# Attention remade ahead of two expert layers: transposes of both heads at once, a mask added by TensorE, other loads and another step order

## The chip, the cores and the metric

The kernel runs on one core of a Trainium2 chip. The core has five engines that run their own instruction lists in order and meet only at semaphores: TensorE (PE, with its weight loads as PEld), VectorE (DVE), ScalarE (ACT), GpSimd (POOL) and SyncE (SP), which here issues every DMA. The metric is the device time of one execution in microseconds. The kernel before takes 1068.88 us (median of 3 runs, 1068.88 to 1069.41).

## The reference

Three layers follow each other; the change touches the first and the beginning of the second.

```python
# attention: batch 2, 8 heads, 576 positions, head size 64
q_d, k_d, v_d = (x.reshape(B, H, S // 4, 4, D).mean(axis=3) for x in (q, k, v))
out_up = np.repeat(softmax(q_d @ k_d.T / 8) @ v_d, 4, axis=2)        # coarse part
scores = np.where(abs(i - j) < 4, q @ k.T / 8, -1e9)                 # local part: a band 7 wide
x = out_up + softmax(scores) @ v                                     # 1152 tokens of 512 numbers
# 8 experts, all of them for every token, weights P from 8 rounds of row and column scaling
for e in range(8): out += P[:, e:e + 1] * (np.maximum(x @ w1[e], 0) @ w2[e])   # 512 -> 1024 -> 512
# last layer, mish between two products: 512 -> 2048 -> 512
```

## The kernel before, in words

Products that matter for precision are made of f16 pairs: a number is scaled by a power of two, cut into a high and a low f16 half, and each product takes three matmuls (high by high, high by low, low by high). So every weight matrix is first measured (a maximum over it gives the scale), then split into halves.

Attention works on pairs of heads, four pairs to a batch, numbered 0 to 3 in batch 0 and 4 to 7 in batch 1. For a pair the steps are: load q, k, v (`LQ`, `LV`) and 128 overlapping windows of v (`LW`); transpose q and k with TensorE (`TP`, line 501) and copy them from PSUM to the layout `qt`, `kt` (`TE`, line 514, on ACT); sum groups of four columns (`SQ`, `SK`); the local scores as 24 little products for a window of 24 queries each (`QL`); the coarse scores (`QD`, line 544); mask and maximum (`MK`, on DVE); subtract, exponentiate, sum and divide (`SUB`, `EL`, `LS`, `LN`); transpose in 32 by 32 blocks (`TR`) and spread into a block diagonal `bd` (`BD`); the same for the coarse part (`DM`, `ED`, `DS`, `DN`, `AP`, `AE`); the products with v (`AV`, `AD`); the sum of both parts, scaled (`UP`, `XF`), and its two f16 halves in `x` (`XH`, `XL`).

All instructions stand in an order written out by hand: the string `ORDER` is a list of such step names with their arguments, and each step issues its instructions to its engines when its name comes. Between the steps of attention stand those of the first expert: `W` for the measuring and splitting of w1 of expert 0 (`first_gen`: eight reduces on DVE at line 175, then for eight pieces a scaling on DVE at 191, the high half on ACT at 192 and the low half on POOL at 193), `Y` for w2 of expert 0, `Z` for measuring w1 of expert 1, `GP` for the gate's weights. When batch 0's `x` is there, the first expert begins on it: `M` (12 matmuls, line 757, into one of two PSUM banks), `R` (ACT empties the bank, line 763), `H` (DVE makes both halves of `h`, lines 768 and 769), and then `N` (its second product, line 790).

So three stages can be told apart in what follows. Stage 1 runs from the start to the first `M`: attention of batch 0 and the split of w1. Stage 2 runs from there to the end of `ORDER`: the first expert on batch 0 beside the attention of batch 1. Stage 3 is the first expert's first product on batch 1, with the gate in it. After that come the remaining experts and the last layer, which the change does not touch.

Of the kernel before, what the change touches and what calls it, by code (L numbers as in the profile page):

```python
# [10 lines left out]
F32 = mybir.dt.float32  # L11
# [10 lines left out]
def attn_moe_moe2_kernel(ctx: ExitStack, tc: tile.TileContext, q, k, v, w_gate, w1, w2, w_in, w_out, out):  # L22
    nc = tc.nc
# [16 lines left out]
    HSC2 = 2.0 ** -26  # L40
    CW = 512
# [70 lines left out]
    max_ps = [None]  # L112

    def all_max_gen(m):

        if not max_ps[0]:
            ma = all_max(m)
            yield
            yield
            return ma  # L120
        ma = Max(m, max_ps[0]())
        yield
        ma.row()
        yield
        return ma.spread()

# [31 lines left out]
    class Split:  # L158


        def __init__(self, name, srcs, slot, spare=0):
            self.name, self.srcs, self.slot, self.spare = name, srcs, slot, spare
            self.raw = []

        def load(self):
            for src in self.srcs:
                r = rawp.tile([128, 2048], F32, tag="raw", name="raw")
                nc.sync.dma_start(out=r.rearrange("p (a b) -> p a b", a=src.shape[1]), in_=src)
                self.raw.append(r)

        def scale_gen(self):
            mx = sm.tile([128, 8], F32, tag="mx", name="mx")
            for i, r in enumerate(self.raw):
                for c in range(4):
                    nc.vector.tensor_reduce(out=mx[:, 4 * i + c:4 * i + c + 1], in_=r[:, c * 512:(c + 1) * 512],
                                            axis=AX.X, op=ALU.max, apply_absolute_value=True)
                    yield
            m1 = sm.tile([128, 1], F32, tag="m1", name="m1")
            nc.vector.tensor_reduce(out=m1, in_=mx, axis=AX.X, op=ALU.max)
            ma = yield from all_max_gen(m1)  # L180
            self.s, self.inv = scale_from_max(ma, "sc_" + self.name, self.spare)
            yield

        def first_gen(self):

            self.tiles()
            yield from self.scale_gen()
            for i in range(8):
                o = slice(i * 512, (i + 1) * 512)
                rr = self.raw[i // 4][:, (i % 4) * 512:(i % 4 + 1) * 512]  # L190
# [3 lines left out]
                yield  # L194
            self.raw = []
# [5 lines left out]
        def split_gen(self):  # L201
# [16 lines left out]
            self.raw = []  # L218
# [151 lines left out]
    def w1_split(e):  # L370

        return (SplitSq if e > 1 else Split)(f"w1_{e}", [w1[e, i * 256:(i + 1) * 256, :].rearrange("(k p) f -> p k f", p=128)
                                 for i in range(2)], "wa", 2)

    def w2_split(e):

        return (Split if e == 0 else SplitSq)(f"w2_{e}", [w2[e, i * 512:(i + 1) * 512, :].rearrange("(k p) d -> p k d", p=128)
                                 for i in range(2)], "wb")


    ident = const.tile([128, 128], F32, name="ident")
    ones = const.tile([128, 128], F32, name="ones")
    ss = const.tile([128, B, 2 * NP], F32, name="ss")
# [6 lines left out]
    acc = accp.tile([128, NTT, DM], F32, name="acc")  # L390
    w_in32, w_out32 = w_in.bitcast(I32), w_out.bitcast(I32)
# [6 lines left out]
    def emit_consts(mask):  # L398
        make_identity(nc, ident)
        nc.vector.memset(ones, 1.0)  # L400
        nc.vector.memset(ss, 0.0)
        nc.gpsimd.memset(mask, 0.0)
        for j in range(4):
            for g0, g1, off in ([(0, 1, 0), (1, G, 3)] if j == 0 else
                                [(0, G - 1, 3), (G - 1, G, 8)] if j == 3 else [(0, G, 3)]):
                mk = mask[32 * j:32 * j + 32, g0:g1, :]

                nc.gpsimd.affine_select(out=mk, in_=mk, pattern=[[0, g1 - g0], [1, 32]], compare_op=ALU.is_ge,
                                        fill=-8e9, base=3 - off, channel_multiplier=-1)
                nc.gpsimd.affine_select(out=mk, in_=mk, pattern=[[0, g1 - g0], [-1, 32]], compare_op=ALU.is_ge,  # L410
                                        fill=-8e9, base=3 + off, channel_multiplier=1)


    xs = [None, None]

    class Attention:
# [4 lines left out]
        def load_m(self, src, j, tag, name):  # L421

            t = self.p[tag].tile([HM, 2, 2, 4, D], F32, tag=tag, name=name)
            nc.sync.dma_start(out=t.rearrange("p h a r d -> p (h a) (r d)"),
                              in_=src[self.b, 2 * j:2 * j + 2].rearrange("h (a p r) d -> p (h a) (r d)", a=2, r=4))
            return t

        def load_qk(self, j):
            self.qm[j] = self.load_m(q, j, "qk", "qm")
            self.km[j] = self.load_m(k, j, "qk", "km")  # L430

        def load_vm(self, j):
            self.vm[j] = self.load_m(v, j, "vm", "vm")

        def load_vw(self, j):
# [4 lines left out]
            vb = v[self.b, 2 * j:2 * j + 2]  # L440

            def win(jj, i0, i1):
                base = v[self.b, 2 * j, 0:32, :]
                src = bass.AP(tensor=base.tensor, offset=base.offset + (24 * jj - 3 + 96 * i0) * D,
                              ap=[[D, 32], [96 * D, i1 - i0], [1, D]])
                nc.sync.dma_start(out=tv[32 * jj:32 * jj + 32, i0:i1, :], in_=src)


            win(0, 1, 2 * G)
            win(3, 0, 2 * G - 1)  # L450
            win(1, 0, 2 * G)
            win(2, 0, 2 * G)
            nc.sync.dma_start(out=t[0:32, :, 0, :], in_=vb[:, 0:32, :].rearrange("h s d -> s h d"))
            nc.sync.dma_start(out=t[96:128, :, G - 1, :], in_=vb[:, S - 32:S, :].rearrange("h s d -> s h d"))
# [3 lines left out]
        def VSQ(self, j):  # L458
            vv = self.vm[j].rearrange("p h a r d -> p h (a r d)")
            junk = self.p["w2"].tile([HM, 512], F32, tag="w2", name="junk")  # L460
            for i in range(2):
                nc.scalar.activation(out=junk, in_=vv[:, i, :], func=AF.Square,
                                     accum_out=ss[0:HM, self.b, 2 * j + i:2 * j + i + 1])

        def VP(self, j):
            t = self.vm.pop(j)
            v2 = self.p["w2"].tile([HM, 512], F32, tag="w2", name="v2")
            v2 = v2.rearrange("p (h a r d) -> p h a r d", h=2, a=2, r=2)
# [9 lines left out]

        def VSM(self, j):
            self.vmax.row()  # L480

        def VSB(self, j):
            b = self.b

# [857 lines left out]
```

## Time and profile before

| | us |
|---|---|
| median of 3 runs | 1068.88 |
| the profiled execution | 1070.91 |
| its span, first to last instruction | 1069.1 |
| PE busy in the span | 1019.4 |
| DVE busy | 608.2 |
| ACT busy | 508.6 |
| POOL busy | 74.8 |

The span is the profiled execution without the 1.8 us around it. Of the span all but the first four of forty slices show PE busy at nine tenths or more, so what an edit in the first part is worth has to be read from that part alone. Times below count from the start of the span. A row that names a releaser after an arrow says what ended the idle time in front of an instruction.

### The profile page before, as it was taken

To read this page: it belongs to the slowest core of one execution; us is meant where nothing else is said; L and a number is where in the kernel's file an instruction comes from. 1 tells how busy PE (TensorE), PEld (TensorE's weight loads), DVE (VectorE), ACT (ScalarE), POOL (GpSimd) and SP (SyncE) were. 2 spreads that over 40 slices of the span, in tenths; PEclk is the share of its full clock that TensorE was granted. 3 is DMA by queue.
4 is the path that set the end of the run, shared out by engine and by line. 5 is a ranking of instruction groups with operands and counts; after the bars stand their busy time and mean duration, and the time that the engine had idled before them with its cause. 6 is when DMAs were issued, how large, how long until landed. Compare 5 with 4: busy or idle time off the path is not lost.

```text
span 1069.1 us, 18210 instructions
## 1 busy us (share of the span) xinstructions
PE 1019.4 (95%) x7545; PEld 695.5 (65%) x7545; DVE 608.2 (57%) x1312; ACT 508.6 (48%) x907; POOL 74.8 (7%) x102
## 2 busy tenths in 40 slices
PE   3777899999998999999999999999999999999998
PEld 2555656667447746754774675477467566888897
DVE  3686893732575376458338645654864336555541
ACT  5867742327526633762663475266437222334431
POOL 2463240000000000000000000000000000000000
PEclk9558899999999999999999999999999999999999
DMA  7637210200451244215123521412320440200010
GB/s 189 123 57 165 56 40 2 67 13 1 158 190 47 79 126 131 79 39 199 30 80 96 170 79 41 158 60 79 117 90 1 174 191 1 80 21 17 6 60 31
DMA packets 70211, 89.40 MB, mean 84 GB/s; under 512 B 16624, under 2 KB 54512, under 8 KB 68848
## 3 DMA queue, kind: packets, MB, share of 16 engines
q1 hardware_dynamic: 70128, 88.24, 26.7%
q8 instruction: 59, 0.97, 0.4%
q14 instruction: 24, 0.20, 0.1%
HBM read 73.29 MB, written 14.94 MB: 83 GB/s over the span
## 4 chain that ended last, share of the span: by engine, by line
PE 73%; DVE 11%; DMA 3%; ACT 3%; issue 2%; POOL 0%; ACTq 0%; POOLq 0%; SPq 0%
PE mm L757 33%; PE mm L790 21%; PE mm L1124 9%; PE n L1191 8%; DMA scr<-st 2%; DVE wal L221 1%; ACT junk L232 1%; DVE acc L805 1%; DVE w L293 1%; DVE w L290 1%; DVE m L297 1%; DMA scri<-st 1%; DVE w L286 1%; DVE w L284 1%; DVE h L769 1%
## 5 line engine op out<-in xcount | busy, mean ns | idle before, releaser
L757 PE MATMUL mm<-x,wah 128*128 128x288 f16 x2048 | 383.1, 289 | 9.2 <-ACT r L763 5.6
L790 PE MATMUL mm<-wbh,h 128*128 128x512 f16 x1152 | 350.6, 379 | 0.0
L757 PE MATMUL mm<-x,wal 128*128 128x288 f16 x1024 | 295.4, 288 | 0.0
L790 PEld LDWEIGHTS <-h 128*128 128x128 f16 x1728 | 168.2, 98 | 195.0 <-issue 1.1
L757 PEld LDWEIGHTS <-wah 128*128 128x128 f16 x2048 | 201.3, 99 | 64.1 <-issue 10.3
L790 PE MATMUL mm<-wbl,h 128*128 128x512 f16 x576 | 218.3, 379 | 0.2 <-DVE wbl L221 0.2
L781 DVE TENSOR_TENSOR h<-rr,h 128x1152 f16<-128x1152 f32 x49 | 66.5, 1358 | 152.8 <-ACT h L783 152.8
L779 ACT ACTIVATE rr<-mm 128x288 f32<-128x288 f32 x224 | 90.5, 407 | 121.2 <-PE mm L757 120.4
L757 PEld LDWEIGHTS <-wal 128*128 128x128 f16 x1024 | 101.1, 99 | 26.5
L1124 PE MATMUL mm<-xc,win 128*128 128x256 f16 (+1 forms) x960 | 107.6, 262 | 0.0
L1124 PEld LDWEIGHTS <-win 128*128 128x128 f16 x960 | 87.2, 98 | 13.3
L1133 ACT ACTIVATE tt<-mm,cf 128x512 f32<-128x512 f32 (+1 forms) x40 | 25.8, 645 | 113.1 <-PE mm L1124 111.3
L1140 DVE TENSOR_TENSOR tt<-tt 128x128 f32<-128x128 f32 x128 | 31.6, 288 | 68.8 <-ACT tt L1133 67.7
L783 ACT ACTIVATE h<-rr 128x1152 f16<-128x1152 f32 x56 | 65.0, 1161 | 1.5
L94 POOL PARTITION_ALL_REDUCE ma<-m x25 | 11.4, 454 | 701.1 <-DVE m L236 419.6
L232 ACT ACTIVATE junk<-raw 128x1024 bf16<-128x1024 f32 x52 | 54.5, 1048 | 5.4 <-DMA raw<-in_moe_w_dram 5.4
L805 DVE SCALAR_TENSOR_TENSOR acc<-mm,pc,acc 128x512 f32<-128x512 f32 x63 | 45.9, 745 | 6.5 <-PE mm L790 6.3
L1191 PEld LDWEIGHTS <-g 128*128 128x128 f16 x432 | 42.1, 98 | 5.0
L221 DVE SCALAR_TENSOR_TENSOR wbl<-raw,sc_w,wbh 128x1024 f16<-128x1024 f32 x32 | 40.6, 1306 | 0.0
L322 DVE TENSOR_TENSOR st<-w,st 128x512 f16<-128x512 f32 x32 | 22.1, 690 | 32.5 <-ACT st L321 32.0
L321 ACT ACTIVATE st<-w 128x512 f16<-128x512 f32 x32 | 19.3, 621 | 42.6 <-DMA scr<-st 37.4
L272 ACT ACTIVATE w<-f 128x512 f32<-128x512 f32 x32 | 20.8, 668 | 36.0 <-DMA f<-in_moe_w_out_dram 35.4
(188 smaller groups left out, 1069.1 us busy)
## 6 DMA issues: line engine op xcount, KB each, us to landing
raw<-in_moe_w_dram SPq DMA_DIRECT2D x32, 1024.0 KB
f<-in_moe_w_in_dram SPq DMA_DIRECT2D x16, 512.0 KB
f<-in_moe_w_out_dram SPq DMA_DIRECT2D x16, 512.0 KB
scr<-st SPq DMA_DIRECT2D x32, 256.0 KB
scri<-st SPq DMA_DIRECT2D x16, 256.0 KB
win<-scri SPq DMA_DIRECT2D x2, 2048.0 KB
qm<-in_q_dram SPq DMA_DIRECT2D x8, 288.0 KB
km<-in_k_dram SPq DMA_DIRECT2D x8, 288.0 KB
```

The source lines that it names most:

```text
L221: nc.vector.scalar_tensor_tensor(out=self.lo[:, o], in0=rr, scalar=self.s, in1=self.hi[:, o], op0=ALU.mult, op1=ALU.subtract)
L232: nc.scalar.activation(out=junk, in_=r[:, c * 1024:(c + 1) * 1024], func=AF.Square, accum_out=mx[:, 2 * i + c:2 * i + c + 1])
L757: nc.tensor.matmul(self.ps, lhsT=wt[:, ws], rhs=x[:, xi, kk, o:o + CH], start=(n == 0), stop=(n == 3 * KT - 1))
L779: nc.scalar.activation(out=r[:, c * CH:(c + 1) * CH], in_=g.ps, func=AF.Relu, scale=HSC)
L781: nc.vector.tensor_tensor(out=low[1][:, 1, :], in0=low[0], in1=low[1][:, 0, :], op=ALU.subtract)
L783: nc.scalar.activation(out=h[ft][:, 0, :], in_=r, func=AF.Copy)
L790: nc.tensor.matmul(ps, lhsT=h[ft][:, hi, t * 128:(t + 1) * 128], rhs=wt[:, ws], start=(ft == 0 and n == 0), stop=(ft == FT - 1 and n == 2))
L805: nc.vector.scalar_tensor_tensor(out=a, in0=ps, scalar=pc[:, t:t + 1], in1=a, op0=ALU.mult, op1=ALU.add)
L1124: nc.tensor.matmul(ps[:, q_ * n:(q_ + 1) * n], lhsT=win[q_][:, wi, f, ws], rhs=x[:, xi, kk, :], start=(m == 0), stop=(m == 3 * KT - 1))
L1133: nc.scalar.activation(out=tt[:, 0:2 * n], in_=ps, func=AF.Mish, scale=coef[c][:, f:f + 1])
L1140: nc.vector.tensor_tensor(out=a[o], in0=a[u], in1=a[v], op=op)
L1191: nc.tensor.matmul(ps, lhsT=gt(c, f)[:, gi, a, :], rhs=wout[b][:, wi, f, :], start=(k == f == n == 0), stop=(k == len(terms) - 1 and f == ...
```

## The change

What it does:

- Loads of q and k: four DMAs of a quarter each in place of one, into a tile of 72 rows that holds the two heads of a position beside each other, so one transpose turns both heads (`load_qk`). Each piece that a DMA moves is then 256 bytes long; before it was 1 KB.
- `TP` writes its four transposes into PSUM columns that stand four apart, so that the result lies in the order of positions. `TQ` (ACT) and `TK` (ACT or DVE) then copy 288 neighbouring numbers; `TE` is gone.
- The mask is made by DVE with arithmetic; the identity too, without the `affine_select` of POOL. It is added by a bf16 matmul of the identity with the mask, into which the 24 little products accumulate; `MK`'s addition goes. `SUB` becomes `SU` on DVE, straight from PSUM. `kt` has three zero columns in front and five behind.
- Windows of v run on into the next head (the mask closes them), so the two extra DMAs at the edges (lines 453 and 454) go.
- w1 and w2 of expert 0 and w1 of expert 1 are measured by squares on ACT, in quarters; the split of w1 is an ACT and a DVE instruction for each quarter.
- Steps name their engine (`:A`, `:V`, `:G`); `H` makes the high half of two chunks at once and `I` the low half; scratch tiles lie in `acc` and `h`.
- `ORDER` is another list.

What it moves. The first place is ACT at the start of attention, after its table load. The names `qt` and `kt` are the transposed tiles, `ad` the coarse softmax. Before:

```order
L514 ACTIVATE qt_183<-at 64x2x2x72 x2
L514 ACTIVATE kt_185<-at 64x2x2x72 x4
L514 ACTIVATE qt_183<-at 64x2x2x72 x2
L514 ACTIVATE qt_184<-at 64x2x2x72 x4
L514 ACTIVATE kt_186<-at 64x2x2x72 x4
L462 ACTIVATE junk,ss<-vm 72x512 x2
L620 ACTIVATE ad,dsu<-at,dnm 72x144 x4
```

Now, at the same place:

```order
L536 ACTIVATE qt_133<-at 128x288 x2
L439 ACTIVATE kt_135<-at 64x288 x2
L439 ACTIVATE kt_136<-at 64x288 x3
L536 ACTIVATE qt_134<-at 128x288
L645 ACTIVATE ad,dsu<-at,dnm 72x144 x4
```

Sixteen strided copies stood ahead of the first exponentials; now there are eight contiguous ones, and part of the `kt` copies is on DVE.

The second place is DVE at the end of stage 1, from the largest value of w1 to the `xf` of the fourth pair. Before:

```order
L179 TENSOR_REDUCE m_848<-mx 128x1
L683 SCALAR_TENSOR_TENSOR xf<-at,sx_607,up 128x288 x2
L106 TENSOR_REDUCE mrow<-at 1x1
L63 TENSOR_SCALAR mc<-at 128x1
L65 TENSOR_SCALAR ei<-mc 128x1
L71 TENSOR_SCALAR ab<-ei 128x1
L72 TENSOR_SCALAR ab<-ei 128x1
L73 TENSOR_SCALAR sc_w_0_880<-ab 128x2
L191 TENSOR_SCALAR raw<-raw,sc_w_0_880 128x512 x3
L587 STREAM_TRANSPOSE atl<-sl 128x384
L598 COPY bd_191<-atl 32x12x24 x2
L191 TENSOR_SCALAR raw<-raw,sc_w_0_880 128x512 x4
```

Now, from the scale of w1 (`sc_w_0`) on, with `wal` its low half:

```order
L75 TENSOR_SCALAR sc_w_0_803<-ab 128x2
L619 STREAM_TRANSPOSE acc<-sl 128x384
L441 COPY kt_135<-at 64x288 x2
L441 COPY bd_141<-acc 32x12x24 x2
L222 SCALAR_TENSOR_TENSOR wal<-raw,sc_w_0_803,wah 128x1024
L706 SCALAR_TENSOR_TENSOR xf<-at,sx_686,h 128x288 x2
L222 SCALAR_TENSOR_TENSOR wal<-raw,sc_w_0_803,wah 128x1024 x2
L706 SCALAR_TENSOR_TENSOR xf<-at,sx_686,h 128x288 x2
L222 SCALAR_TENSOR_TENSOR wal<-raw,sc_w_0_803,wah 128x1024
```

The scale of w1 is now there before the third pair's `xf`, one pair earlier, and the eight scalings and eight POOL subtractions are four DVE instructions.

The third place is DVE at the beginning of stage 3, where `gx`, `L` and `m` belong to the gate, whose maximum TensorE turns next. Before:

```order
L768 CAST h<-r 128x288
L769 TENSOR_TENSOR h<-r,h 128x288
L840 TENSOR_SCALAR gx<-invx,sc_wg 128x9
L841 TENSOR_REDUCE L<-lp 128x72
L842 TENSOR_TENSOR L<-L,gx 128x72
L844 TENSOR_REDUCE m_2122<-L 128x1
L768 CAST h<-r 128x288
```

Now:

```order
L887 TENSOR_SCALAR gx<-invx,sc_wg 128x9
L888 TENSOR_REDUCE L<-lp 128x72
L889 TENSOR_TENSOR L<-L,gx 128x72
L891 TENSOR_REDUCE m_2025<-L 128x1
L807 TENSOR_TENSOR h<-r,h 128x576
```

No half of `h` stands ahead of the gate's maximum any more.

The diff, cut to its core:

```diff
-        def load_m(self, src, j, tag, name):
...
-            nc.sync.dma_start(out=t.rearrange("p h a r d -> p (h a) (r d)"),
-                              in_=src[self.b, 2 * j:2 * j + 2].rearrange("h (a p r) d -> p (h a) (r d)", a=2, r=4))
+        def load_qk(self, src, j):
+
+            t = self.p["qk"].tile([HM, 2, 4, 2, D], F32, tag="qk", name="qk")
+            for a in range(2):
+                for h in range(2):
+                    nc.sync.dma_start(out=t[:, a, :, h], in_=src[self.b, 2 * j + h, 288 * a:288 * a + 288]
+                                      .rearrange("(p r) d -> p r d", r=4))
...
-            for a in range(2):
-                for i in range(2):
-                    c = (2 * a + i) * HM
-                    nc.tensor.transpose(ps[:, c:c + HM], t[:, par, a, 2 * i:2 * i + 2, :].rearrange("p r d -> p (r d)"),
-                                        ident[0:HM, 0:HM])
...
+            ps = self.at()[:, 0:288]
+            o = ps.rearrange("c (p r) -> c r p", r=4)
+            for r in range(4):
+                nc.tensor.transpose(o[:, r, :], t[:, i, r].rearrange("p h d -> p (h d)"), ident[0:HM, 0:HM])
...
+        def TQ(self, j, i):
+            nc.scalar.activation(out=keep["qt"][j % 2][:, 288 * i:288 * i + 288], in_=self.st["T", j, 0, i],
+                                 func=AF.Copy, scale=QSC)
+
+        def TK(self, j, i, h, eng):
+            c = slice(64 * h, 64 * h + 64)
+            copy_on(eng, keep["kt"][j % 2][c, h, 3 + 288 * i:291 + 288 * i], self.st["T", j, 1, i][c])
...
+                nc.tensor.matmul(sl[:, 0:384], lhsT=ident16, rhs=mask.rearrange("p g h c -> p (g h c)"), start=True,
+                                 stop=False)
...
-                                 rhs=kt[:, :, k0:k0 + 32], start=True, stop=True, tile_position=(0, 32 * jj))
+                                 rhs=kt[:, :, 24 * n:24 * n + 32], start=False, stop=(n >= 20),
+                                 tile_position=(0, 32 * jj))
...
-            nc.sync.dma_start(out=t[0:32, :, 0, :], in_=vb[:, 0:32, :].rearrange("h s d -> s h d"))
-            nc.sync.dma_start(out=t[96:128, :, G - 1, :], in_=vb[:, S - 32:S, :].rearrange("h s d -> s h d"))
...
-                nc.vector.tensor_scalar(out=rr, in0=rr, scalar1=self.s, scalar2=None, op0=ALU.mult)
-                nc.scalar.activation(out=self.hi[:, o], in_=rr, func=AF.Copy)
-                nc.gpsimd.tensor_tensor(out=self.lo[:, o], in0=rr, in1=self.hi[:, o], op=ALU.subtract)
...
+            if eng == "A":
+                nc.scalar.activation(out=spare_act, in_=r, func=AF.Square, accum_out=self.mx[:, i:i + 1])
...
+        def high(self, i):
+            if not hasattr(self, "hi"):
+                self.tiles()
+            nc.scalar.activation(out=self.hi[:, i * 1024:(i + 1) * 1024], in_=self.quarter(i), func=AF.Copy,
+                                 scale=self.s)
...
-        make_identity(nc, ident)
...
+        nc.vector.transpose(out=row, in_=col)
+        nc.vector.tensor_tensor(out=d, in0=col, in1=row, op=ALU.subtract)
+        for i in range(4):
+            p = slice(32 * i, 32 * i + 32)
+            nc.vector.tensor_scalar(out=ident[p, p], in0=d[p, :], scalar1=0.0, scalar2=None, op0=ALU.is_equal)
...
-        "LQ0 TP0.1 TP0.3 LQ1 TP0.2 TP0.0 TE0.1 TE0.3 LV0 TP1.2 TE0.2 TE0.0 LV1 LQ2 SK0 SQ0 TP1.1 TP1.3 TP1.0 QL0.0 "
...
+        "LQ0 LK0 LK1 TP0.0.1 TP0.0.0 TQ0.1 TQ0.0 LK2 TP0.1.0 SQ0:V TP0.1.1 TK0.0.1:A TK0.0.0:V TK0.1.0:A TK0.1.1:V "
...
```

## Rows read from the trace of the kernel before

**Rows 1.** Stages: us, length, busy us (instructions) of each engine, PE clock, DMA, GB/s:

```profile
0.00:11.33 11.33, 0.00 (x0) 0.00 (x0) 3.44 (x9) 1.28 (x1) 0.73 (x7) 1.00 0.67 156
11.33:80.15 68.82, 49.35 (x470) 36.31 (x470) 45.71 (x112) 51.62 (x119) 33.87 (x43) 0.63 0.54 118
80.15:166.00 85.85, 76.25 (x703) 48.18 (x702) 67.27 (x146) 55.41 (x129) 28.14 (x27) 0.90 0.32 82
166.00:196.93 30.93, 28.66 (x283) 22.42 (x282) 17.29 (x63) 7.12 (x17) 0.00 (x0) 0.94 0.01 2
196.93:1069.10 872.17, 865.17 (x6095) 588.58 (x6092) 474.45 (x985) 393.12 (x642) 12.06 (x27) 1.00 0.25 83
```

**Rows 2.** Waits of PE in stage 1: us in total, times, longest:

```profile
PE at L501 <- POOL ident masks.py:199: 11.3, 1, 11.3
PE at L661 <- ACT bd L596: 5.0, 2, 3.7
PE at L669 <- ACT atd L651: 1.7, 2, 1.2
PE at L501 <- ACT kt L514: 1.5, 1, 1.5
```

**Rows 3.** POOL by line, up to 169 us:

```profile
L193 POOL TENSOR_TENSOR wal<-raw,wah 128x512 f16<-128x512 f32 x8 | 9.7, 1231 | 2.3 <-ACT wah L192 2.3
...
masks.py:199 POOL TENSOR_SCALAR_AFFINE_SELECT ident<-ident 128x128 f32<-128x128 f32 x1 | 0.3, 283 | 10.1 <-issue 10.1
```

**Rows 4.** PE in order of time: start, us, line, tiles, [idle before, releaser]:

```profile
17.73 1.08 PE L537 MATMUL at<-kt,qt 128*32 128x64 f32 x32 [2.04 <-ACT qt L514]
...
80.15 0.69 PE L757 MATMUL mm<-x,wah 128*128 128x288 f16 x2
```

**Rows 5.** Waits of PE in stage 2:

```profile
PE mm L757 <- ACT r L763: 5.6, 3, 2.4
PE at L102 <- DVE mv L476: 3.0, 1, 3.0
```

**Rows 6.** Waits of PE in stage 3:

```profile
PE gm L102 <- DVE m L844: 2.3, 1, 2.3
```

**Rows 7.** ACT by line, stage 1: instructions, busy us, mean ns, idle before:

```profile
L514 ACT ACTIVATE kt<-at 64x288 f32<-64x288 f32 x20 | 13.6, 681 | 0.4
L514 ACT ACTIVATE qt<-at 64x288 f32<-64x288 f32 x16 | 10.8, 678 | 10.4 <-PE at L501 10.1
```

**Rows 8.** ACT by line, stage 2, and the page's row of another measuring:

```profile
L763 ACT ACTIVATE r<-mm 128x288 f32<-128x288 f32 x16 | 6.5, 410 | 8.0 <-PE mm L757 4.8 <-DVE h L769 2.5 <-ACT r L763 0.3
...
L232 ACT ACTIVATE junk<-raw 128x1024 bf16<-128x1024 f32 x52 | 54.5, 1048 | 5.4 <-DMA raw<-in_moe_w_dram 5.4
```

**Rows 9.** DMA from 2 to 6 us: packets, and share of 16 engines:

```profile
DMA packets 762, 0.76 MB, mean 189 GB/s; under 512 B 24, under 2 KB 762, under 8 KB 762
q1 hardware_dynamic: 762, 0.76, 75.3%
```

**Rows 10.** DMA from 57 to 63 us:

```profile
DMA packets 2063, 0.91 MB, mean 151 GB/s; under 512 B 1560, under 2 KB 2062, under 8 KB 2062
q1 hardware_dynamic: 2062, 0.89, 88.6%
```

**Rows 11.** DVE by line, stage 2:

```profile
L769 DVE TENSOR_TENSOR h<-r,h 128x288 f16<-128x288 f32 x16 | 13.6, 848 | 0.6
L768 DVE CAST h<-r 128x288 f16<-128x288 f32 x16 | 7.2, 449 | 1.4 <-ACT r L763 1.4
```

**Rows 12.** PE by line, stage 1:

```profile
L544 PE MATMUL at<-kd,qd 128*72 128x288 f32 x16 | 8.5, 668 | 2.0 <-DVE sl L552 1.2 <-DVE kd L524 0.7
L501 PE MATMUL at<-ident,km 72*128 72x72 f32 x48 | 8.2, 334 | 1.6 <-ACT kt L514 1.5
```

**Rows 13.** DMA from 20 to 26 us, mostly w1:

```profile
q1 hardware_dynamic: 993, 2.04, 98.6%
```

**Rows 14.** Waits of SP's own queue, up to 170 us:

```profile
SPq L453 <- DMA vw<-in_v_dram: 24.6, 8, 5.0
```

More of the change, by code (lines that the diff above doesn't have):

```diff
@@ L184, in first_gen @@
[L184 to L190, printed above, removed]
-                nc.vector.tensor_scalar(out=rr, in0=rr, scalar1=self.s, scalar2=None, op0=ALU.mult)
-                nc.scalar.activation(out=self.hi[:, o], in_=rr, func=AF.Copy)
-                nc.gpsimd.tensor_tensor(out=self.lo[:, o], in0=rr, in1=self.hi[:, o], op=ALU.subtract)
-                yield
-            self.raw = []
+            self.parts = {}
@@ new lines, in load_part, with measure @@
+        def load_part(self, i):
+            r = rawp.tile([128, 2048], F32, tag="raw", name="raw")
+            src = self.srcs[i]
+            nc.sync.dma_start(out=r.rearrange("p (a b) -> p a b", a=src.shape[1]), in_=src)
+            self.parts[i] = r
+            if len(self.parts) == 2:
+                self.raw = [self.parts[0], self.parts[1]]
+        def load(self):
+            for i in range(2):
+                self.load_part(i)
+        def measure(self, i, eng):
+            if not hasattr(self, "mx"):
+                self.mx = sm.tile([128, 4], F32, tag="mx", name="mx")
+                self.squares = eng == "A"
+            r = self.quarter(i)
+            if eng == "A":
+                nc.scalar.activation(out=spare_act, in_=r, func=AF.Square, accum_out=self.mx[:, i:i + 1])
+            else:
+                nc.vector.tensor_reduce(out=self.mx[:, i:i + 1], in_=r, axis=AX.X, op=ALU.max,
+                                        apply_absolute_value=True)
@@ new lines, in quarter, with bound, scale @@
+        def quarter(self, i):
+            return self.parts[i // 2][:, i % 2 * 1024:(i % 2 + 1) * 1024]
+        def bound(self):
+            m1 = sm.tile([128, 1], F32, tag="m1", name="m1")
+            nc.vector.tensor_reduce(out=m1, in_=self.mx, axis=AX.X, op=ALU.add if self.squares else ALU.max)
+            return m1
+        def scale(self, ma):
+            f = scale_from_squares if self.squares else scale_from_max
+            self.s, self.inv = f(ma, "sc_" + self.name, self.spare)
+        def high(self, i):
[3 more added lines that the diff above has]
+                                 scale=self.s)
@@ L197, in tiles, with low_part @@
+        def low_part(self, i):
+            self.low(self.quarter(i), slice(i * 1024, (i + 1) * 1024))
         def tiles(self):
@@ L400, in emit_consts @@
         nc.vector.memset(ones, 1.0)
         nc.vector.memset(ss, 0.0)
[L402 to L411, printed above, removed]
+        nc.vector.tensor_scalar(out=far, in0=d, scalar1=-3.0, scalar2=None, op0=ALU.add)
@@ L414, in attn_moe_moe2_kernel, with copy_on @@
+    spare_up = []
+    def copy_on(eng, out, in_):
+        if eng == "A":
+            nc.scalar.activation(out=out, in_=in_, func=AF.Copy)
+        else:
+            tensor_engine(eng).tensor_copy(out=out, in_=in_)
     xs = [None, None]
@@ new lines, in load_vw, with VQ @@
+            n = 2 * G
+            start, end = self.b == j == 0, self.b == B - 1 and j == NP - 1
+            if start:
+                nc.vector.memset(tv[0:32, 0, :], 0.0)
+                win(0, 0, 1, p0=3)
+            if end:
+                nc.vector.memset(tv[96:128, n - 1, :], 0.0)
+                win(3, n - 1, n, p1=27)
+            win(0, int(start), n)
+            win(1, 0, n)
+            win(2, 0, n)
+            win(3, 0, n - int(end))
+        def VQ(self, j):
+            t = self.vm[j]
+            nc.scalar.activation(out=spare_act[0:HM, :], in_=t.rearrange("p h a r d -> p (h a r d)"), func=AF.Square,
+                                 accum_out=ss[0:HM, self.b, j:j + 1])
@@ L972, in attn_moe_moe2_kernel @@
                 g1[ft, c].relu()
-                g1[ft, c].parts()
+                if c == 3:
+                    g1[ft, c].high("A")
+                    g1[ft, c].low()
                 tick()
```

364 lines of the change are left out of this document (169 added, 195 removed), and 47 rows, old and new, of the table ORDER.

## The prediction

> **What bounds the kernel now.** First the busy times by stage [rows 1]: from 197 us to the end PE works 865.2 of 872.2 us. That part runs instructions that the change leaves alone, so it can't be won from, and any shift ahead of it comes out at the end one for one. The change lies in the first 197 us, and there no engine is full: in stage 1 ACT works 51.6 of 68.8 us, PE 49.4, DVE 45.7, POOL 33.9; in stage 2 PE works 76.3 of 85.9, DVE 67.3, ACT 55.4. These stages are held by waits between engines, and by PE's clock, granted at 0.63 of full in stage 1 and 0.90 in stage 2.
>
> Then PE's waits, since PE carries the chain afterwards. It starts at 11.3 us, when POOL has made the identity [rows 2], and POOL stood 10.1 us in front of that instruction with no other engine named [rows 3]. After that the largest waits of stage 1 end with ACT: 5.0 us for `bd`, 1.7 for `atd`, 1.5 for `kt` [rows 2] and 2.0 for `qt` [rows 4]. In stage 2 they are 5.6 us for `R`, ACT's emptying of the bank, and 3.0 us for DVE's `mv` [rows 5]; in stage 3 one of 2.3 us for the gate's maximum on DVE [rows 6].
>
> So ACT is what to look at next. In stage 1 its copies out of the transposes are 36 instructions and 24.4 us [rows 7], nearly half its work, at 0.68 us for 288 elements to a partition with a stride in what they write. The same number of elements without a stride takes it 0.41 us at line 763 [rows 8].
>
> **The start.** The identity now comes from some 20 small instructions of DVE, which is free from 0.8 us. POOL's 10.1 us in front of its first work of that kind will come before its first product of attention instead, where nothing is asked of it yet; it costs nothing unless POOL is wanted before 15 us. PE then waits for q and k. A packet of 1 KB cost 0.753 x 4 x 16 / 762 = 0.063 us of one DMA engine [rows 9]. In the other stretch [rows 10] 1560 packets were small and 503 others; with those at 0.063 the small ones come to (85.1 - 31.7) / 1560 = 0.034 us. One q or k of a pair is 288 packets of 1 KB before, 1.1 us of the sixteen engines, and 1152 packets of 256 bytes now, 2.45 us. With the stream beginning at about 2 us, q0 is there near 5, k0 near 7.5 and k1 near 10 (an estimate). The first local product, at 17.73 us before [rows 4], stands in PE's order behind the transposes of k1, so it comes at about 11.
>
> **The rest of stage 1.** From the first local product to the first `M` at 80.15 [rows 4] it was 62.4 us: PE waited 68.8 - 49.4 - 2.0 = 17.5 and worked 44.9.
> - ACT: up to the first `M` there are now 12 `TQ` and 11 `TK`, contiguous, at 0.41 us: 9.4 in place of 24.4. Added are four measurings of w1 by squares, 1.05 us each by the like of line 232 [rows 8], 4.2. ACT ends near 41 us of work. 11 `TK` go to DVE; I price them at 0.41 (bounds 0.3, under the cast of 288 elements, 0.45 [rows 11], and 0.5): 4.6 us, against the eight reduces of line 175 and the eight scalings of line 191 that DVE loses. DVE stays near 46.
> - The split of w1 was the tail: scaling on DVE, high half on ACT, low half on POOL at 1.23 us for each of eight pieces [rows 3], begun when the fourth pair's `bd` and `xf` were still to come. It now begins one pair earlier and leaves POOL out. The 5.0 us for `bd` belong to this tail.
> - PE gets work: two parts of `QL4`, 1.1 us [rows 4]; `QD4`, a quarter of line 544's 8.5, 2.1 [rows 12]; five mask matmuls, priced by the two matmuls of 288 columns that take 0.69 us at 80.15 [rows 4], so 0.46 for 384 columns: 2.3. Together 5.5 us.
> - The mask's addition and `SUB` become two DVE instructions on PSUM; POOL's 0.8 us hop goes out of the local chain. I count it in the waits.
>
> Of the waits I let the 8.2 us that end with ACT go, and leave 9.3: the engines that end them are no freer than before. Sum: 11 + 44.9 + 5.5 + 9.3 = 70.7. I take 70 for the first `M`, ten earlier.
>
> DMA has to keep up with that. Up to q5, whose transposes stand before the first `M`, SP issues 13 q or k (31.9 us), five v (5.6), five sets of windows of 1536 small packets (16.3) and w1 (5.9 [rows 13]): 59.7 us of all engines. Begun at 2 us and never idle, that ends at 62. SP's 24.6 us behind the windows [rows 14] go, since nothing is written twice any more. It fits, with 6 to 8 us to spare.
>
> **Stage 2.** It was 85.9 us, 76.3 of work and 9.6 of waits. PE loses the 3.2 us of `QL4` and `QD4` done before, 2.2 at this stage's clock, and gets three mask matmuls, 1.0. The waits for `R` came from ACT's strided copies and from DVE's `H`, 1.3 us for each of sixteen chunks [rows 11], in front of the next `R`; these halves are now made for two chunks at once, so I take 5.6 down to 2.5 and the 3.0 for `mv` to 0.5. Against that the measuring of w2 and of expert 1's w1, eight instructions of 1.05 us, stands in ACT's queue ahead of `R`; I count it inside the 2.5. With fewer waits the share of time at the lower clock shrinks; from 0.90 to 0.93 is 2.5 us of 76. So 85.9 - 1.2 - 5.6 - 2.5 = 76.6: nine earlier.
>
> **Stage 3.** The 2.3 us go: `H` no longer stands ahead of the gate's maximum. With half a microsecond of clock after it, 2.8.
>
> **Sum.** 10 + 9 + 3 = 22 us. The profiled execution took 1070.9 with a span of 1069.1 and so would take 1049; against the median of 1068.9 the forecast is 1047.
>
> **A price that no row shows.** The transposes now write PSUM columns four apart. A group of four costs 8.2 / 12 = 0.68 us now [rows 12], written without gaps. The nearest rows with and without a gap are ACT's, 0.68 against 0.41 us for 288 elements [rows 7, 8], 1.66 times. With the same factor the 32 groups would cost 32 x 0.45 = 14 us more, half of it beside waits. Below nothing is excluded: the same columns are written. I take nothing, as the nearest operation is the transpose itself, and keep 14 for the range. The Trainium skill speaks against the change here: by the page "SBUF — State Buffer", section "Door 1: The DMA port swizzle", PSUM lies in lines of 8 bytes and any pattern with gaps slows matmuls significantly. It gives no factor, and no row here shows a matmul that writes with gaps; by the rule the sum would end in the last rival below.
>
> **The rivals.**
> - DMA holds stage 1. For it speaks that the small packets raise its work to 59.7 us and that SP issues in order: the windows of the fourth pair wait for a buffer that the first pair's product frees, and q, k and w1 queue behind them. Against it: the waits at lines 453 and 454 go. If the engines are kept busy 0.78 of the time, the last needed transfer ends near 78; two us are won there, and the total is 2 + 9 + 3 = 14, so 1055.
> - The new order closes more of the gaps. Stage 1 then ends at its DMA bound, 62, and stage 2 comes to 70, little over its work at full clock (76.3 x 0.90 = 69). That is 18 + 16 + 3 = 37, so 1032. For it: ACT and DVE then have 41 and 46 us of work in 57.
> - Only the start is won. PE at the lower clock was already busy 72% of stage 1; what ACT frees is taken by the 5.5 us of new work, and stage 2 keeps its waits behind the measuring on ACT. 4 + 0 + 3 = 7, so 1062; with nothing won at the start either, no change.
> - Slower: the transposes. Place: line 501's successor, 32 groups of four, 23 of them before the first `M`. About 13 us of extra time would hide in what waits are left (9.3 and 4). So the gain of 22 is gone when the groups cost 35 us more, 1.1 each, that is at 2.6 times their present 0.68. At four times it is 32 x 2.04 = 65, less 13, so 52 more than the forecast: 1099.
>
> **How the numbers follow.** Forecast 0.47, its own range 1038 to 1055; DMA 0.20; fewer gaps 0.16; only the start 0.05; no change 0.03; slower 0.09. A measurement of this kernel tells 0.2%, about 2 us, from no change. So faster 0.88, same 0.03, slower 0.09. The range from 1028 to 1065 leaves out the best of the third case and the slower one, less than two in ten.
>
> **What would show it.** Right: the first `M` at 66 to 74 us, the copies of 288 elements at about 0.41 us on ACT, no wait of SP behind windows of v, stage 2 under 80 us, no wait before the gate's maximum. Wrong: transposes above 1 us for a group of four (the price without a row); PE's waits in stage 1 that end with a DMA (the first rival); a first `M` before 64 us, or ACT's measuring as what `R` waits for.

## The result, and the profile after

The changed kernel takes 1056.65 us (median of five, 1055.0 to 1060.9) beside 1068.88 for the kernel before: a ratio of 0.9896, interval 0.9868 to 0.9924. It is faster by 12 us, or 1.0%, where 22 us were forecast. On a second chip it was 1053.45, ratio 0.9849 (0.9828 to 0.9871). The profiled execution took 1060.9 with a span of 1059.1, at the upper end of the five; its parts are therefore compared with the trace of before by itself.

The stages of the changed kernel, with the columns of [rows 1]: up to PE's first instruction, up to the first `M`, up to the end of the written-out order, up to the first product of line 830 in the fifth tile, and the rest.

```profile
0.00:6.19 6.19, 0.00 (x0) 0.03 (x1) 4.97 (x21) 1.28 (x1) 3.81 (x15) 1.00 0.23 53
6.19:77.62 71.43, 49.02 (x507) 34.05 (x508) 45.12 (x105) 36.96 (x98) 28.64 (x33) 0.67 0.60 140
77.62:152.42 74.80, 70.30 (x673) 43.91 (x672) 51.85 (x132) 43.02 (x109) 18.18 (x23) 0.97 0.29 86
152.42:179.86 27.44, 26.71 (x282) 21.70 (x281) 12.50 (x41) 12.08 (x25) 0.00 (x0) 1.00 0.01 2
179.86:1059.10 879.24, 868.36 (x6096) 590.03 (x6093) 473.96 (x981) 393.55 (x643) 12.02 (x27) 1.00 0.25 82
```

Against [rows 1] the first `M` comes 2.5 us earlier (77.62 for 80.15), where ten were forecast. Stage 2 is 11.1 shorter (forecast 9), stage 3 is 3.5 shorter (forecast 3). The rest, which was to stay as it is, is 7.1 longer. Sum: 10.0, the difference of the spans. ([rows 1] cut the kernel before at 196.93; its first product of the fifth tile begins at 196.77. Like for like, stage 3 is 3.3 shorter and the rest 6.9 longer.) So two terms are to be explained, stage 1 and the rest.

What PE waits for in the changed kernel up to the end of stage 3 (us in total, times, longest), the largest:

```profile
PE at L532 <- DMA qk<-in_q_dram: 16.5, 6, 6.2
PE at L532 <- DMA qk<-in_k_dram: 3.9, 3, 2.6
PE mm L789 <- ACT r L798: 3.8, 4, 2.9
PE at L686 <- ACT ad L645: 2.4, 1, 2.4
```

The waits for ACT that the forecast let go, for `bd`, `atd` and `kt` [rows 2], are nearly gone: `kt` has 0.7, `bd` now waits 1.5 for POOL, and one of 2.4 for `ad` is new. Of the 20.4 us for q and k the first 6.2 are the start, where PE waited 11.3 us for the identity before. The other 14.2 have no like in [rows 2], and the forecast named such waits as the sign of its first rival.

The forecast counted from the first local product, so the changed kernel is read from there too. PE in order of time (start, us, line, tiles, idle before and what ended it), then the stretch from that product to the first `M`, with the columns of the stages:

```profile
12.76 1.19 PE L532 MATMUL at<-ident,qk 72*128 72x72 f32 x8 [2.55 <-DMA qk<-in_k_dram]
...
14.20 0.66 PE L570 MATMUL at<-kt,qt 128*32 128x64 f32 x16
```

```profile
14.20:77.62 63.42, 44.96 (x483) 30.95 (x483) 41.60 (x98) 34.72 (x93) 28.64 (x33) 0.63 0.63 146
```

PE works 45.0 us there, where the forecast had 44.9 + 5.5 = 50.4, and waits 18.5, where the forecast left 9.3. Of the 18.5, 10.3 end with a load of q. One line of its products got cheaper, the first with v, before and now (instructions, busy us, mean ns, idle before):

```profile
L661 PE MATMUL at<-bd,vw 128*64 128x96 f32 x96 | 10.3, 360 | 6.2 <-ACT bd L596 5.0 <-DMA vw<-in_v_dram 1.2
```

```profile
L686 PE MATMUL at<-bd,vw 128*64 128x96 f32 x96 | 8.0, 328 | 3.9 <-ACT ad L645 2.4 <-POOL bd L441 1.5
```

ACT's copies out of the transposes, line by line in stage 1:

```profile
L439 ACT ACTIVATE kt<-at 64x288 f32<-64x288 f32 x11 | 4.4, 402 | 6.5 <-PE at L532 5.4 <-DVE kt L441 1.0
...
L536 ACT ACTIVATE qt<-at 128x288 f32<-128x288 f32 x11 | 4.2, 404 | 15.0 <-PE at L532 14.9
```

0.40 us each, as forecast (0.41), against 0.68 [rows 7]. The transposes, which now write PSUM columns four apart, in order of time, before and now, both at a granted clock of 0.5:

```profile
54.23 0.74 PE L501 MATMUL at<-ident,km 72*128 72x72 f32 x4
```

```profile
59.18 0.74 PE L532 MATMUL at<-ident,qk 72*128 72x72 f32 x4
```

Written without gaps, a group took 0.68 us on average [rows 12], and 0.69 to 0.74 at the same lower clock. The gaps cost nothing, and the last rival of the forecast falls: the rule on gaps in PSUM that the Trainium skill gives on its page "SBUF — State Buffer", section "Door 1: The DMA port swizzle", doesn't show in these matmuls.

Now the waits for q and k. The DMA engines in the first 20 us (2 to 20 us: packets, share of 16 engines):

```profile
DMA packets 6300, 1.55 MB, mean 86 GB/s; under 512 B 6300, under 2 KB 6300, under 8 KB 6300
...
q1 hardware_dynamic: 6300, 1.55, 38.0%
```

They are idle more than half of the time, so they aren't what holds q and k back. One such packet takes 0.38 x 18 x 16 / 6300 = 0.0174 us of an engine here; the forecast took 0.034, from a mixture [rows 10]. SP's own queue in order of time, first in the kernel before, then in the second trace of the changed one (start, us, line, tile, number of DMAs):

```profile
0.72 0.43 SPq L424 DMA_DIRECT2D qm<-in_q_dram  x1
1.20 0.36 SPq L424 DMA_DIRECT2D km<-in_k_dram  x1
```

```profile
0.73 3.54 SPq L455 DMA_DIRECT2D qk<-in_q_dram  x4
4.31 9.97 SPq L455 DMA_DIRECT2D qk<-in_k_dram  x12
...
64.75 3.33 SPq L455 DMA_DIRECT2D qk<-in_q_dram  x4
```

A tile of q or k used to keep SP busy for 0.4 us. It now keeps it busy for 3.3, four DMAs of 0.83. Thirteen such tiles stand ahead of the first `M`: 43 us of SP's queue, with five sets of windows (2 us each) and w1 in the same queue. SP issues without a pause worth naming until q5 at 64.75, whose transposes PE waits for.

In the middle of stage 1 it is not the price of an issue alone. In the first trace four DMAs of windows took 6.7 us from 37.8 on and a tile of k 6.5 from 44.7 on, and the DMA engines, which move w1 then, were busy 0.87 to 1.02 of the time from 36 to 50 us. There the queue probably stood behind the engines; no run takes that apart. In the changed kernel no wait of SP behind windows of v is left, against 24.6 us [rows 14].

### The profile page after: what moved, and what is told of

It reads as the page before. It is cut to its first block, busy times and chain, and to the rows that moved or that the text cites. A ratio compares the mean times of both kernels' runs of the same rounds, so it can differ in the third digit from the quotient of the medians.

```text
span 1059.1 us, 18183 instructions
## 1 busy us (share of the span) xinstructions
PE 1014.4 (96%) x7553; PEld 689.7 (65%) x7553; DVE 588.4 (56%) x1279; ACT 486.9 (46%) x874; POOL 62.6 (6%) x97
## 4 chain that ended last, share of the span: by engine, by line
PE 76%; DVE 9%; DMA 7%; ACT 3%; SPq 2%; issue 2%; POOL 0%; ACTq 0%; POOLq 0%
PE mm L789 33%; PE mm L830 22%; PE mm L1186 9%; PE n L1253 8%; DMA scr<-st 2%; DMA raw<-in_moe_w_dram 2%; SPq L455 2%; DVE wal L222 1%; PE at L686 1%; DVE acc L845 1%; DVE w L294 1%; DVE w L291 1%; DVE m L298 1%; DMA scri<-st 1%; ACT junk L233 1%
## 5 line engine op out<-in xcount | busy, mean ns | idle before, releaser
L96 POOL PARTITION_ALL_REDUCE ma<-m x25 | 11.3, 453 | 710.5 <-DVE m L237 426.2
L222 DVE SCALAR_TENSOR_TENSOR wal<-raw,sc_w,wah 128x1024 f16<-128x1024 f32 x32 | 41.1, 1292 | 0.0
```

The costliest lines, as they stand in the source:

```text
L222: nc.vector.scalar_tensor_tensor(out=self.lo[:, o], in0=rr, scalar=self.s, in1=self.hi[:, o], op0=ALU.mult, op1=ALU.subtract)
```

## The experiments

**Theory "issue":** stage 1 goes at the pace at which SP issues the DMAs of q and k. **Rivals:** "engines" (the small packets themselves are slow, the forecast's first rival as it was worded) and "chain" (products, ACT and DVE set the pace, the waits for q and k only fill slack).

**1. One tile, cut in other ways.** Each tile of q and k is loaded in one of several forms:

```diff
+            elif form == "half":
+                for a in range(2):
+                    nc.sync.dma_start(out=t[:, a], in_=bass.AP(
+                        tensor=base.tensor, offset=base.offset + a * 288 * D,
+                        ap=[[4 * D, HM], [D, 4], [S * D, 2], [1, D]]))
+            elif form == "quarter":
+                for a in range(2):
+                    for r in range(4):
+                        nc.sync.dma_start(out=t[:, a, r], in_=...)
...
```

> The changed kernel with its q and k loads cut in different ways, tile by tile; every tile still gets 1152 packets of 256 bytes. As is: 4 DMAs of 288 packets, which the trace after shows as 0.83 us each on SP's queue. Others: 2 DMAs of 576, 8 of 144 (cut by row, or by pairs of rows), 16 of 72, and 4 of 288 issued by ACT's and by POOL's queue. Theory 'issue': stage 1 of the changed kernel goes at the pace at which SP issues these DMAs (16 engines only 0.38 busy in the first 20 us). Then SP's time per tile differs between the forms: if it goes by the packet every tile stays near 3.3 us whatever the cut; if it goes by the DMA, 2 DMAs cost about 1.7 us, 8 cost 2.5 to 6.6 and 16 cost 5 to 13; if the two sides' unequal shape is what is slow (the windows of v, of equal shape, take 0.5 us for 384 packets), the cuts by row cost 0.2 to 0.3 each. Theory 'engines' (the forecast's first rival as it was worded): the packets themselves are slow, every tile needs 3.3 us between its first and last packet in all forms, the ACT and POOL queues too. The total of this kernel is of no interest.

SP's queue, in order of time; L499 is the form as changed, L469 two DMAs of 576 packets, L475 eight of 144 cut by row, L482 sixteen of 72, L494 eight of 144 cut by pairs of rows:

```profile
7.67 1.64 SPq L469 DMA_DIRECT2D qk<-in_k_dram  x2
9.35 3.31 SPq L499 DMA_DIRECT2D qk<-in_k_dram  x4
12.78 1.65 SPq L469 DMA_DIRECT2D qk<-in_q_dram  x2
14.53 3.61 SPq L475 DMA_DIRECT2D qk<-in_k_dram  x8
...
52.78 7.24 SPq L482 DMA_DIRECT2D qk<-in_q_dram  x16
...
90.15 3.36 SPq L494 DMA_DIRECT2D qk<-in_q_dram  x8
```

The same 1152 packets cost 1.64, 3.31, 3.61, 3.36 or 7.24 us. (The other tile of L475, of L482 and of L494 took longer: 5.3, 11.5 and 5.4.) A DMA of 576 packets costs 0.82, as does one of 288, so between these the price goes by the DMA and not by the packet. One of 72 or 144 costs 0.42 to 0.45. The shape by itself doesn't make the difference: in L494, as in L499, the rows of a partition lie back to back in DRAM and apart in SBUF, and it costs 0.42. What sets the price between 144 and 288 packets stays open. By "engines" the cut would not have mattered; experiment 5 settles it for the whole kernel. On ACT's queue four DMAs took 3.9 and 3.2 us, on POOL's 3.2 and 2.9.

**2. The first two tiles of k from ACT's queue.**

```diff
+            queue = nc.scalar if src is k and self.b == 0 and j < 2 else nc.sync
...
-                    nc.sync.dma_start(out=t[:, a, :, h], ...)
+                    queue.dma_start(out=t[:, a, :, h], ...)
```

> The changed kernel, with the first two loads of k (8 DMAs) issued from ACT's queue, which has nothing to do before 7.9 us, instead of SP's. Same packets, same DMA engines. Theory 'issue': two queues issue side by side, SP's later loads all come 6.6 us earlier, the first local product stands at 9.5 to 11 in place of 14.2, the first M at 71 to 73 in place of 77.6, and the time falls by 4 to 6.5 us, to 1050 to 1053. Theory 'engines': nothing moves by more than 1 us. Theory 'chain' (the products, ACT and DVE set the pace and the waits for q and k only show where the slack is): the first product is earlier, the first M is not, by more than 2 us; time within 2 us.

1048.85 us, ratio 0.9790 (0.9749 to 0.9831). Its four executions lie between 1043.0 and 1052.8, so the size of the gain is known only roughly. In the trace the first `M` came at 69.9, 6 to 8 us earlier than in the two traces of the changed kernel (77.6 and 76.1), the first local product at 12.1:

```profile
12.07 0.66 PE L571 MATMUL at<-kt,qt 128*32 128x64 f32 x16
...
69.89 0.69 PE L790 MATMUL mm<-x,wah 128*128 128x288 f16 x2
```

Same packets, same DMA engines: only the queue that issues them was relieved. "Chain" is out too.

**3. The identity by POOL, as before.**

```diff
-        nc.vector.memset(ident, 0.0)
+        make_identity(nc, ident)
...
-            nc.vector.tensor_scalar(out=ident[p, p], in0=d[p, :], scalar1=0.0, ...)
```

> The changed kernel with the identity made by POOL again, as before (the rest of the start as changed). It would be there at about 11.4 us and not at 6.2. By the forecast's term for the start the first local product and all behind it come about 4 to 5 us later: 1061. Theory 'issue': k1 lands at 12.7 anyway, so the transposes of q0 and k0 only move into a time in which PE waits; the first local product comes at 14.5 to 15.5 and the time rises by 0 to 1.2 us.

1053.92, ratio 0.9837 (0.9807 to 0.9866), beside 0.9849 and 0.9896 for the changed kernel: no loss. PE starts at 12.2 us instead of 6.2, but the first local product comes at 15.6, 1.4 later, and the first `M` at 74.8, if anything earlier. The forecast's gain at the start was hidden behind the late k.

**4. The windows of v written twice, as before.**

```diff
+            nc.sync.dma_start(out=t[3:32, :, 0, :], in_=vb[:, 0:29, :].rearrange("h s d -> s h d"))
+            nc.sync.dma_start(out=t[96:123, :, G - 1, :], in_=vb[:, S - 27:S, :].rearrange("h s d -> s h d"))
```

> The changed kernel with two small DMAs behind each set of windows of v, which write the first and the last window once more with the same values, so that SP waits there for the windows to land as it did before (24.6 us in eight waits). Theory 'issue': SP's queue is what stage 1 goes by, so each of the five sets ahead of q5 costs its wait (about 3 us) and two issues (0.65 us): the first M comes 12 to 18 us later, the time rises to 1067 to 1074, and it takes most of what the change won. Theory 'chain': the stream has slack, the first M moves by under 5 us.

1073.94, ratio 1.0043 (1.0025 to 1.0061). The first `M` came at 88.8, stage 2 took 79.7. SP's waits up to there:

```profile
SPq L492 <- DMA vw<-in_v_dram: 9.2, 6, 4.8
SPq L493 <- DMA vw<-in_v_dram: 6.6, 6, 1.6
```

These 15.8 us, and the issues beside them, cost 16 to 21 us at the end: without this part the change would have won nothing.

**5. Two DMAs for a tile.** The form of 1.64 us everywhere, with the changed kernel beside it on the same chip:

```diff
-            for a in range(2):
-                for h in range(2):
-                    nc.sync.dma_start(out=t[:, a, :, h], in_=src[self.b, 2 * j + h, 288 * a:288 * a + 288]...)
+            for a in range(2):
+                nc.sync.dma_start(out=t[:, a], in_=bass.AP(tensor=base.tensor, offset=base.offset + 288 * a * D,
+                                                           ap=[[4 * D, HM], [D, 4], [S * D, 2], [1, D]]))
```

> The changed kernel as it is, on the chip of the three kernels beside it, as their measure: 1054 to 1061, 0.985 to 0.992 of the time before. Its trace also tells whether the part behind stage 3 (code that the change leaves alone, 872.3 us in the one trace of before, 879.2 in the one of after) is longer each time: if that was chance it comes near 873 here, if it belongs to the changed kernel, 876 or more.

> The changed kernel with every tile of q or k loaded by two DMAs of 576 packets (both heads at once) instead of four of 288; the same packets to the same places. One such DMA also takes SP 0.82 us, so a tile costs 1.64 us of its queue instead of 3.3. Theory 'issue': the 13 tiles ahead of the first M give SP 21 us back; the first local product comes at 9 to 11 us, the waits for q and k (20 us in stage 1) shrink to under 8, the first M comes at 64 to 69 where the forecast had it, and the time is 1042 to 1049. Theory 'engines': the same packets, nothing changes, 1054 to 1060. Theory 'chain': waits for q and k turn into waits for ACT and DVE, the first M stays above 74, time over 1053.

1038.71 us (1036.85 to 1039.24), ratio 0.9712 (0.9695 to 0.9730), against 1053.45 for the changed kernel: 14.7 us from nothing but the cut of the loads. Its stages:

```profile
5.31:63.06 57.75, 45.67 (x507) 32.02 (x508) 47.43 (x112) 39.50 (x103) 32.19 (x34) 0.72 0.87 183
63.06:133.12 70.06, 68.88 (x672) 43.34 (x671) 51.87 (x130) 40.93 (x104) 16.61 (x22) 0.99 0.27 82
```

What PE waits for in it up to the first `M`, of q and k:

```profile
PE at L532 <- DMA qk<-in_k_dram: 1.6, 1, 1.6
PE at L532 <- DMA qk<-in_q_dram: 1.3, 1, 1.3
```

The first local product comes at 10.7 (forecast 11), the first `M` at 63.1. The waits for q and k after the start are down from 14.2 us to 2.9, and the DMA engines work 0.87 of stage 1 instead of 0.60. They are near to being the next limit; the second kernel of 6 and the last of 7 point that way.

**6. Two DMAs for a tile, with an identity by POOL, or with k0 and k1 from ACT's queue.** The edits are those of 2 and 3.

> As the one with two DMAs per tile, and the identity by POOL again, there at about 12 us. With SP's queue holding stage 1 that cost nothing. Theory 'cover' (the identity was hidden only by the late k): now q0, k0 and k1 are there by 8 us, so the first local product comes 4 to 6 us later than with the identity by DVE, and a part of that, 2 to 5 us, arrives at the end. If something later in stage 1 (SP's stream, w1's split) sets the first M, under 1 us arrives.

> Two DMAs per tile, and the first two tiles of k issued by ACT's queue beside SP's. Theory 'issue': SP's stream moves another 3.3 us ahead, the first local product 1 to 3 us; if SP's queue still is what stage 1 goes by, the first M and the time move by 2 to 3.5 us, if the queue has slack by now, by under 1.5 us. It may be the fastest of all.

The identity by POOL now costs 7.1 us (1045.85): PE starts at 12.1 and the first `M` comes at 70.8, 7.7 later. The same edit cost nothing in 3. It is more than was expected (2 to 5), and more than the 4.8 by which the first local product moved (15.5 for 10.7); where the other 3 us arise was not taken apart.

The ACT queue, worth some 5 us in 2, now loses 2.6 (1041.30), which neither expectation had. ACT issues until 4.8 us and copies q0 only at 6.9 (6.1 without). But what the first local product waits for (12.0 instead of 10.7) is k1, which lands later, without and with ACT's queue:

```profile
9.21 1.22 PE L532 MATMUL at<-ident,qk 72*128 72x72 f32 x8 [1.56 <-DMA qk<-in_k_dram]
```

```profile
10.57 1.22 PE L533 MATMUL at<-ident,qk 72*128 72x72 f32 x8 [2.25 <-DMA qk<-in_k_dram]
```

With two queues the DMA engines were busy 0.91 and 1.00 of the time from 4 to 6 and from 6 to 8 us, without the second 0.74 and 0.73. So k1 probably shares them there with tiles that are needed later.

**7. Parts of the change undone, each on the kernel with two DMAs for a tile.** The halves of h by chunk, the mask by DVE, and the sums of q4 by DVE:

```diff
         def high(self, eng):
-            copy_on(eng, self.both(0), pair_r[self.ft])
+            for n in range(2):
+                o = slice(n * CH, (n + 1) * CH)
+                copy_on(eng, self.both(0)[:, o], pair_r[self.ft][:, o])
```

> The kernel with two DMAs per tile (1038.7), with the high and low halves of h made per chunk of 288 again, in the same places (32 instructions more on DVE and ACT). The forecast laid 5 us of stage 2 and the 2.3 us of stage 3 to making them for two chunks at once: then stage 2 goes from 70.1 to 73 to 75, stage 3 from 27.4 to 28 to 30, and the time to 1042 to 1045. Theory 'order' (the relus come free because of the new order of steps and of ACT's shorter copies): under 1 us more in both, 1038 to 1040.

```diff
-                nc.tensor.matmul(sl[:, 0:384], lhsT=ident16, rhs=mask.rearrange("p g h c -> p (g h c)"), ...)
...
+            nc.vector.tensor_tensor(out=s, in0=self.st.pop(("sl", j))[:, 0:384],
+                                    in1=mask.rearrange("p g h c -> p (g h c)"), op=ALU.add)
```

> The kernel with two DMAs per tile, with the mask added by DVE into the copy of the scores (one more instruction of 384 elements, about 0.55 us, for each pair of heads) and not by TensorE (eight products of 0.43 us less). If PE's work is what counts there, stage 1 gives up to 2.4 us and stage 2 1.0 us back: 1035 to 1038. If the chain of a pair over DVE counts (maximum, difference, exponential, sum), or DVE is short of time beside w1's low parts, it is 1 to 4 us slower: 1040 to 1043.

```diff
-  SQ4:G QL4.0
+  SQ4:V QL4.0
```

> The kernel with two DMAs per tile, with the sums of q for the fifth pair made by DVE in one instruction of about 0.75 us and not by POOL in two, which PE waits 3.4 us for just ahead of the first M (POOL's and DVE's instructions also take twice their usual time there, side by side). If that wait is what the first M stands on, 2 to 3.4 us go: 1035 to 1037. If w1's low parts on DVE or the loads of q5 end next to it, under 1 us: 1038 to 1039.

| kernel | us | ratio to before, interval | first `M` | stage 2 | stage 3 |
|---|---|---|---|---|---|
| two DMAs | 1038.71 | 0.9712 (0.9695 to 0.9730) | 63.1 | 70.1 | 27.4 |
| halves by chunk | 1042.47 | 0.9740 (0.9717 to 0.9763) | 65.0 | 72.2 | 27.1 |
| mask by DVE | 1041.20 | 0.9729 (0.9706 to 0.9752) | 65.2 | 71.4 | 27.4 |
| q4's sums by DVE | 1037.85 | 0.9695 (0.9673 to 0.9717) | 61.8 | 71.9 | 27.4 |

The first row stands on another chip than the others, so the ratios are to be compared. No row is clear of the first by its interval. The halves by chunk show 2 us in stage 2, less than half of what the forecast laid to them and less than the 3.4 by which stage 2 differs between the two traces of the changed kernel (74.8 and 71.4), and nothing in stage 3. The mask costs about the same on either engine, as far as the intervals tell. With q4's sums on DVE the wait of 3.4 us for them is gone, and one of 4.5 for q's DMA is there in its place.

**8. The kernel before once more**, for its trace.

> The kernel before once more, for its trace. The part behind stage 3 took 872.3 us there, with 3.5 us of waits of PE for the last sum of an expert (2.7, 0.4 and 0.5 at its three places), and 874.5 to 879.2 us in all eight traces of changed kernels, with 5.5 to 7.6. If that comes with the change, this trace has 872 to 873 us and waits of 3 to 4 again; if it is chance from run to run, 875 to 878 and 5 to 7.

The rest took 874.7 us (1068.4 - 193.68), against 872.3 in the first trace and 874.5 to 879.2 in the twelve traces of changed kernels, where the mean is 876.5. PE's waits there for the last sum of an expert were 3.2, 0.6 and 0.5 us. In the changed kernels the first of the three is 2.6 to 3.2, the third 1.3 to 2.3 in all but one. In total, before, before again and in the first trace of the changed kernel:

```profile
PE mm L757 <- DVE acc L805: 3.5, 3, 2.7
```

```profile
PE mm L757 <- DVE acc L805: 4.3, 3, 3.2
```

```profile
PE mm L789 <- DVE acc L845: 7.6, 3, 3.1
```

The new trace lies between what the two theories expected. Chance makes 2 us or more of the difference. By the means 3 us come with the change, but two traces of before don't show that.

## Why the prediction was right in sign and too large

- **The start** (first local product at 11): it came at 14.2. The identity was there early, as forecast. The step that failed is "k1 near 10 (an estimate)": k1 landed at 12.8 because SP needed 3.3 us to issue each tile. With two DMAs for a tile it was 10.7.
- **The rest of stage 1** (first `M` at 70): 77.6. By its terms, 11 + 44.9 + 5.5 + 9.3 = 70.7 became 14.2 + 45.0 + 18.5 = 77.7. The copies and the freed waits for ACT came as forecast, and the waits apart from q are 8.2. The other 10.3 are what the sum had not. The step that failed is "Begun at 2 us and never idle, that ends at 62. It fits, with 6 to 8 us to spare". It counted what the packets cost the DMA engines and left out what the DMAs cost the queue that issues them, although that duration stood in the trace for every DMA of before: 0.4 us for a whole tile. Four times that would have been 1.6; that a quarter in the new form costs twice as much as a whole tile before, no row of before shows. The engines were idle 62% of the time from 2 to 20 us. Experiments 1, 2 and 5 show it from three sides. Without this limit the first `M` stood at 63.1 and stage 2 took 70.1, close to the 62 and 70 of the forecast's second rival.
- **PE's work in it** (50.4 from the first local product): 45.0, and that hid a part of the miss. The new work came as priced: by line, the little products, the coarse scores and the mask take 5.3 us more, where 5.5 were added. But the products with v took 12.4 us in place of 16.7 (`L686` for `L661` above is the larger of their two lines). From 40 to 50 us, where some of them stand, PE's granted clock was 0.92 and then 1.00 (near 2.4 GHz), and 0.50 (1.2 GHz) before. The forecast kept the old clock for stage 1.
- **The first rival** had the right place, the right sign (waits that end with a DMA) and nearly the right size, 1055. It had the wrong cause: it spoke of engines busy only 0.78 of the time and of a buffer that comes late. No run shows a buffer as the reason; the waits of SP for buffers up to the first `M` come to 4.7 us, and the engines were busy 0.60 of stage 1. That its 1055 came so near is partly luck: its stage 1 came true, but 1055 has neither the further 2 us won in stage 2 nor the 7 lost in the rest. The main case's own range, 1038 to 1055, misses 1056.65 closely and holds the second chip's 1053.45.
- **Stage 2** (76.6): 74.8, and 71.4 in the second trace. Waits fell from 9.6 us to 4.5, where the forecast had 4. PE's clock went from 0.90 to 0.97, where it had 0.93; PE's work times its clock is the same (68.6 and 68.2), so nearly six of the eleven us are the clock, which rose as the waits went, and five are waits. The two waits that the forecast named shrank: `R` has 3.8 us (1.0 in the second trace) for 5.6, `mv` none. That pairing the halves was a main cause is not borne out (2 us).
- **Stage 3** (three less): 3.5. The wait for the gate's maximum fell from 2.3 [rows 6] to 0.7. It stays away with the halves by chunk as well. What both versions share is the order on DVE: the gate's maximum comes at 155.4 and the first half of `h` at 159.0 (with halves by chunk 140.3 and 143.5), as the forecast had it.
- **The rest** (unchanged): 6.9 longer in this trace, 3.3 in the second pair of traces. The order of the instructions on DVE is the same there, but for the first few. Two things make its length: the three waits for the last sum of an expert, and stretches of 3.4 us at a granted clock of 0.5, which cost half of that, 1.7 us each. Taken off, the rest is 868.2 to 868.9 us in all 14 traces. In the first pair 4.1 us are waits (7.6 for 3.5), and the other 2.8 are about two such stretches, of which the first trace of before has none. What makes the waits longer stays open.
- **The transposes** (0 taken, up to 14 kept): 0.

So in the traces 22 became 10: 7.5 us of it were lost in stage 1 and 6.9 in the rest, and 2.4 more were won in stages 2 and 3. SP's queue cost more than those 7.5, since PE's work came out lower than forecast.

## What to carry to other kernels

The loads here had two prices: what their packets cost the sixteen engines, and what their issue costs the queue that they stand in. Read both in the trace, and add up the second for everything that one queue issues up to the point in question. Of several ways to cut the same load, try the one with the fewest DMAs; here it was worth 14.7 us, nearly as much as all the rest of the change (15.3, 1053.45 for 1068.70 on the same chip). And a part that is worth nothing may only be hidden: the identity by DVE gained nothing with the slow loads and 7 us with the quick ones.

## What was not expected of the hardware

- Issuing one DMA took SP 0.82 us, whether it held 288 or 576 packets of 256 bytes; 0.42 to 0.45 for 72 or 144 packets, 0.5 for the 384 in a DMA of windows, and 0.3 to 0.4 for 288 packets of 1 KB. Neither the number of packets nor the shape tried in experiment 1 accounts for that alone. The Trainium skill, on its page "DMA: Bandwidth & Descriptors", section "Issuing engines are not separate DMA queues", says that starting DMAs from several engines saves only the time to initiate them, "which is usually small relative to the DMA itself". Here the issue was the larger price: 288 packets of 0.0174 us are 5.0 us of an engine, 0.31 us of sixteen, against 0.82 of SP's queue.
- In ten of the twelve traces of changed kernels PE's granted clock fell from 1.0 to 0.5 (2.4 to 1.2 GHz) for 3.4 us once or twice in the rest, each time next to a wait of PE for the last sum of an expert; of the two traces of before, one shows it.
